# Square roots of the first three chunks by arithmetic on VectorE, with a new order of the operations

## The chip, the cores and the metric

The kernel runs on one core of a Trainium2 chip. The metric is the device time of one execution, in microseconds (us). The engines are called PE (TensorE; its weight loads are PEld), DVE (VectorE), ACT (ScalarE) and POOL (GpSimd); SP (SyncE) issues the DMAs. Each engine takes its own queue in program order and waits for others by semaphores.

## What is computed

A gated linear recurrence, followed by a gated convolution unit, over 4 sequences of 6336 tokens with 256 features:

```python
log_a = c * sig_r * np.log(np.clip(a_base, 1e-06, 1.0 - 1e-06))[None, None, :]
a_t = np.exp(log_a)
norm = np.sqrt(np.maximum(1.0 - a_t * a_t, 1e-06))
x_gated = norm * sig_i * x
for t in range(S):
    h = a_t[:, t] * h + x_gated[:, t]
    y[:, t] = h
# then, with x = y:
#   gate = sigmoid(causal convolution of x over 5 tokens, by feature)
#   out  = (gate * (x @ w_val)) @ w_out
```

`sig_r` and `sig_i` are the sigmoids of `r_gate` and `i_gate`. The change is about the square root in the third line.

## The kernel before

The 25,344 tokens are cut into 51 windows (`CHUNKS`, line 16): two of 256 tokens, then 48 of 512, and a last one of 256. Windows go in 28 chunks: chunks 0, 1 and 2 are the single windows 0, 1 and 2 (256, 256 and 512 tokens), and most of the others have two windows, so chunk 3 is windows 3 and 4.

Loads and stores are laid out with tokens on the partitions; the recurrence needs features on the partitions, in two halves of 128 (h = 0, 1). Each window or chunk goes through these steps; the two letters are their names in the order:

- `lr`, `li`, `lx` (L274): SP loads the r gate, the i gate and x of a window, 512 KB each for 512 tokens, into rings of four windows.
- `th` (L289): ACT takes tanh of both gates of a window at once, into `tring`, a ring of three windows. Of its three planes the i gate always lies in plane 1, and the r gate in plane 0 or 2 by turns.
- The i gate with x: POOL by `pp` (L297, adds 1) and `up` (L309, times x), or, for some windows, PE and DVE: `xp` (L314) brings x through PE into PSUM, and `uv` (L323) adds 1 and multiplies on DVE.
- `tr` (L334): PE transposes the r gate, one half of the features at a time; `ex` (L350): ACT takes exp with the feature's factor, which gives `a` in `aring`.
- The square of `a`, in `ering`: `sq` on POOL (L358) or `sa` on ACT (L366).
- `rt` (L377): ACT takes the root of a batch of chunks as Sqrt(0.25 - 0.25 * square), which is half of the norm, without the floor of 1e-6. tanh and exp lie in one table set and Sqrt in another, so ACT loads a table ahead of a batch of roots and another behind it (L509). `BATCHES` (line 19) says which chunks go together: 0, 1 and 2 each alone, then [3, 4], then three chunks at a time, and [26, 27].
- `nt` (L392): PE transposes the roots back; `xg` (L399): DVE multiplies them into the gated x; `xt` (L408): PE transposes the product; `sc` (L430): DVE runs the recurrence along the tokens, by chunk and half.
- Per window: `cv` (L442, the convolution as matmuls), `tg` (L449, tanh of it on ACT), `vl` (L457, x @ w_val), `gv` (L462, the gate on DVE), `ou` (L472, @ w_out), the copy out of PSUM by `cd` on DVE (L480) or `ca` on ACT (L482), and `st` (L493, the store).

The order of all this is the text `ORDER` (line 33), written out in advance: one word per step with the step's window or chunk, its half, and behind `@` the PSUM banks that it uses. A loop at the end (L504) emits the words one by one, so each engine's queue is the words of that engine in this order. Nothing is reordered later. The loop also puts in the table loads, wherever the next word of ACT needs the other set:

```python
table, have = {"th": EXP, "tg": EXP, "ex": EXP, "rt": SQRT}, EXP
if table.get(name, have) != have:
    have = table[name]
    nc.scalar.preload_act_table_set(have)
```

Of the kernel before, what the change touches and what calls it, by code (L numbers as in the profile page):

```python
# [38 lines left out]
s_wl.2 lr.8 li.10 lx.8 xt.2@2,3 xt.1@0,1 sc.1.1 li.9 lr.10 sq.3.0 rt.3 li.11 up.6 sc.1.0 lx.10 lr.11 sc.2.1 sc.2.0
up.5 th.8 lx.11 s_wcast th.10 lx.9 pp.10 up.10 lr.14 th.9 li.13 li.14 lr.13 xp.8@4,5 li.12 lr.12 uv.8 th.11 li.15  # L40
nt.3@0,1 xg.3 nt.4@6,7 pp.11 up.11 cv.1@2,3 tg.1 xg.4 xt.3@0,1 sc.3.1 vl.1@4,5 tr.5.0@6,7 ex.5.0 sq.5.0 tr.5.1@2,3
gv.1 ou.1.0@1 cd.1.0 st.1 lx.12 lr.15 ex.5.1 vl.0@4,5 xp.9@6,7 th.14 sq.5.1 cv.2@2,3 sc.3.0 th.13 uv.9 lx.13 xt.4@1,0
gv.0 ou.0.0@4 cd.0.0 st.0 sc.4.1 lx.15 cv.3@6,7 th.12 li.16 li.18 tr.7.1@4,5 tg.2 vl.2@2,3 gv.2 tg.3 ex.7.1 sq.6.1
sq.6.0 lx.14 pp.14 pp.12 up.12 tr.7.0@6,7 ex.7.0 sq.7.0 lx.16 cv.4@2,3 tg.4 th.15 ou.2.0@4,5 cd.2.0 sc.4.0 st.2 lr.18
lr.16 vl.3@6,7 xp.13@2,3 vl.4@4,5 gv.4 sq.7.1 rt.4 uv.13 th.16 sq.8.1 sq.8.0 pp.15 up.15 li.17 lr.17 up.14 ou.4.0@4,5
li.19 cv.5@0,1 lr.19 gv.3 cd.4.0 lx.17 tg.5 ou.3.0@6,7 lx.18 st.4 cd.3.0 st.3 nt.5@4,5 li.20 xg.5 pp.16 up.16 th.17
pp.17 lr.20 nt.7@6,7 xg.7 lx.19 li.21 nt.6@2,3 xg.6 th.18 pp.18 lr.21 xt.5@4,5 sc.5.1 up.17 vl.5@6,7 cv.6@0,1 tg.6
th.19 tr.9.1@2,3 ex.9.1 li.22 lr.22 up.18 sq.9.1 pp.19 gv.5 sc.5.0 tr.9.0@6,7 ex.9.0 lx.20 ou.5.0@0,1 cd.5.0 sq.10.1
xt.6@5,4 up.19 sc.6.1 cv.7@0,1 tg.7 cv.8@2,3 th.20 lr.24 tg.8 sc.6.0 vl.6@6,7 gv.6 xt.7@0,1 cv.9@4,5 ou.6.0@6,7 sc.7.0
th.21 tg.9 cd.6.0 vl.7@2,3 gv.7 vl.9@6,7 th.22 tr.11.0@0 sc.7.1 ou.7.0@2,3 vl.8@4,5 sq.9.0 tr.12.0@1 gv.9 ou.9.0@6,7  # L50
gv.8 ou.8.0@4,5 sq.10.0 st.5 cd.7.0 cd.9.0 lx.22 st.6 rt.5 lx.21 nt.8@6,7 lr.23 li.23 cd.8.0 nt.9@4,5 pp.22 pp.21
up.22 pp.20 up.20 up.21 xg.8 ex.12.0 xg.9 ex.11.0 li.24 st.7 st.9 li.25 lr.25 lx.23 lx.24 li.26 lr.26 th.23 xt.8@6,7
sc.8.0 sq.11.0 pp.23 sq.12.0 lr.27 li.27 cv.11@2,3 tg.11 cv.10@4,5 sc.8.1 cv.12@0,1 st.8 th.24 pp.24 tg.10 tg.12
vl.11@2,3 tr.11.1@6 ex.11.1 gv.11 vl.10@4,5 gv.10 th.25 xt.9@0,1 sc.9.0 tr.12.1@2 ex.12.1 ou.11.0@6,7 cd.11.0
ou.10.0@4,5 cd.10.0 cv.14@2,3 up.23 lx.25 lx.27 th.26 nt.10@6,7 sc.9.1 st.11 li.29 st.10 tg.14 tr.13.0@4,5 xg.10 up.24
sq.11.1 th.27 ex.13.0 tr.13.1@2,3 vl.12@0,1 gv.12 sq.12.1 li.30 lr.30 lx.26 pp.25 pp.27 sq.13.0 xt.10@6,7 sc.10.1
ex.13.1 sq.13.1 up.27 sq.14.0 pp.26 up.25 lr.28 cv.13@4,5 tg.13 vl.13@0,1 gv.13 li.28 vl.14@2,3 gv.14 ou.12.0@4,5
cd.12.0 ou.13.0@0,1 cd.13.0 ou.14.0@2,3 cv.15@4,5 lr.29 st.13 lx.28 lr.31 sc.10.0 cv.16@0,1 cd.14.0 rt.6 nt.11@6,7
tg.15 tg.16 xg.11 vl.15@2,3 gv.15 th.28 st.12 li.31 lx.29 sq.14.1 up.26 nt.13@4,5 xg.13 pp.28 up.28 nt.12@0,1 xg.12
li.32 vl.16@2,3 gv.16 lx.31 lr.32 lx.30 xt.11@4,5 sc.11.1 sc.11.0 ou.15.0@6,7 th.30 pp.30 th.29 pp.29 cv.18@0,1  # L60
ca.15.0 lr.34 li.34 up.29 cv.17@2,3 tg.18 xt.12@6,7 tg.17 vl.17@0,1 gv.17 tr.15.1@2,3 tr.15.0@4,5 th.31 sc.12.0
ou.17.0@0,1 cd.17.0 sc.12.1 ex.15.1 ex.15.0 cv.20@2,3 tg.20 li.33 lr.33 ou.16.0@0,1 cd.16.0 th.32 vl.18@4,5 gv.18
pp.31 up.31 th.34 xt.13@2,3 sc.13.1 vl.19@6,7 cv.19@0,1 tg.19 gv.19 st.17 st.14 st.16 st.15 up.30 th.33 sq.16.1 lx.32
sc.13.0 li.35 lr.35 lx.33 ou.18.0@4,5 cd.18.0 lx.34 li.36 sq.15.0 lr.38 cv.21@0,1 sq.15.1 vl.21@6,7 st.18 lx.35 lr.36
tg.21 gv.21 vl.20@0,1 sq.16.0 cv.22@2,3 gv.20 li.38 lr.37 li.37 pp.34 ou.19.0@4,5 cd.19.0 pp.33 pp.32 up.32
ou.21.0@6,7 ou.20.0@0,1 rt.7 cd.21.0 st.21 tg.22 cd.20.0 nt.14@4,5 xg.14 st.19 nt.16@6,7 xg.16 vl.22@0,1 gv.22 th.35
up.33 up.34 pp.35 tr.17.1@2,3 ex.17.1 xt.14@4,5 sc.14.0 sc.14.1 tr.17.0@6,7 ex.17.0 cv.23@0,1 cv.24@2,3 tg.23 tg.24
ou.22.0@6,7 cd.22.0 nt.15@0,1 xg.15 vl.24@2,3 vl.23@4,5 gv.23 st.20 st.22 lx.36 gv.24 up.35 cv.26@6,7 sq.17.1 th.36
pp.36 sq.18.0 th.38 xt.15@0,1 sc.15.0 sc.15.1 th.37 pp.37 sq.18.1 sq.17.0 ou.23.0@4,5 tg.26 ca.23.0 cv.25@2,3 tg.25
tr.19.0@6,7 ex.19.0 sq.19.0 xt.16@4,5 sc.16.0 tr.19.1@2,3 ex.19.1 sc.16.1 cv.27@0,1 ou.24.0@6,7 cd.24.0 tg.27  # L70
vl.25@2,3 vl.26@0,1 sq.19.1 rt.8 cv.28@4,5 gv.26 up.36 sq.20.1 li.39 st.23 lx.38 lr.40 pp.38 gv.25 lx.37 vl.27@6,7
gv.27 ou.26.0@0,1 cd.26.0 ou.25.0@2,3 lr.41 lr.39 tg.28 th.39 st.24 cd.25.0 ou.27.0@6,7 cd.27.0 nt.19@0,1 nt.17@2,3
xg.17 xg.19 cv.29@6,7 tg.29 sq.20.0 up.37 up.38 nt.18@4,5 xg.18 vl.28@2,3 gv.28 vl.29@6,7 gv.29 xt.17@0,1 sc.17.1
li.40 th.40 tr.21.1@4 li.41 th.41 pp.40 pp.39 st.26 st.25 tr.21.0@5 ex.21.1 ex.21.0 lx.39 li.42 ou.29.0@6,7 ca.29.0
lr.42 sc.17.0 st.27 lx.40 xt.18@2,3 up.39 th.42 ou.28.0@4,5 cv.30@6,7 cd.28.0 tg.30 tr.22.1@0 ex.22.1 tr.22.0@1
sq.21.0 sq.21.1 up.40 cv.32@6,7 ex.22.0 sq.22.1 tg.32 sc.18.1 cv.31@4,5 tg.31 lr.43 st.29 sc.18.0 li.43 th.43
vl.30@0,1 vl.31@6,7 gv.30 vl.32@4,5 gv.32 gv.31 ou.30.0@0,1 cd.30.0 xt.19@3,2 sc.19.0 ou.31.0@6,7 sq.22.0 rt.9
ou.32.0@4,5 st.28 cd.32.0 cd.31.0 lr.44 sc.19.1 lx.41 lx.43 lr.45 pp.42 pp.43 pp.41 up.41 li.44 up.43 lr.46 li.46
lx.42 up.42 st.30 cv.33@0,1 li.45 vl.33@4,5 tg.33 st.32 gv.33 nt.21@6,7 th.44 nt.20@0,1 xg.20 lx.45 lr.47 li.48 lr.48
th.46 pp.44 xg.21 nt.22@2,3 xg.22 lx.44 cv.35@4,5 th.45 pp.45 pp.46 up.45 st.31 li.47 ou.33.0@0,1 ca.33.0 tg.35  # L80
xt.20@6,7 sc.20.0 tr.23.1@2,3 ex.23.1 sc.20.1 cv.34@0,1 tg.34 cv.36@4,5 sq.24.1 tg.36 vl.35@2,3 gv.35 vl.36@0,1 gv.36
tr.23.0@6,7 vl.34@2,3 gv.34 ou.35.0@4,5 cd.35.0 lx.46 st.33 up.44 xt.21@0,1 sq.23.1 th.48 pp.48 ex.23.0 sq.24.0
sc.21.0 sc.21.1 th.47 cv.38@2,3 tg.38 ou.36.0@4,5 ou.34.0@6,7 ca.36.0 sq.23.0 ca.34.0 xt.22@2,3 tr.25.0@0 ex.25.0
sc.22.1 sq.25.0 tr.25.1@4 ex.25.1 sc.22.0 cv.37@6,7 tg.37 cv.39@0,1 tg.39 vl.40@4,5 vl.38@6,7 gv.38 sq.25.1 rt.10
st.35 li.49 st.36 vl.37@0,1 st.34 vl.39@2,3 lx.49 lr.49 lr.50 lx.48 gv.37 ou.38.0@6,7 cd.38.0 st.38 gv.39 cv.40@0,1
ou.37.0@6,7 cd.37.0 st.37 lx.47 nt.23@2,3 nt.24@6,7 tg.40 up.46 th.49 ou.39.0@0,1 ca.39.0 xg.23 xt.23@2,3 xg.24
cv.41@6,7 gv.40 ou.40.0@0,1 tg.41 ca.40.0 pp.49 pp.47 sc.23.1 cv.42@4,5 vl.41@0,1 sc.23.0 tg.42 gv.41 tr.26.0@3 li.50
ex.26.0 vl.42@6,7 st.39 up.47 th.50 xt.24@4,5 nt.25@2,3 gv.42 up.48 xg.25 st.40 ou.41.0@0,1 ca.41.0 st.41 cv.43@6,7
# [452 lines left out]
```

## Time and profile before

| | |
|---|---|
| median of 3 runs | 300.46 us (300.38 to 301.98) |
| the profiled execution | 300.32 us |
| its span in the trace | 298.5 us |
| ACT busy | 278.8 us, 93% of the span |
| DVE busy | 247.6 us, 83% |
| PE busy | 246.4 us, 83% |
| POOL busy | 232.8 us, 78% |
| DMA | 104.75 MB, mean 351 GB/s |

The span is the time from the first to the last instruction in the trace; 1.82 us of the execution lie around it. An engine's busy time is the time in which it had an instruction under way. In the profile's second part the span is cut into 40 equal slices, one digit each: the busy share of an engine in tenths. A row of a group gives line, engine, operation, what is written and read with its shape, the count, then busy us and the mean ns of one, then the idle time just before and what ended it. In a timeline, the first number is the start in us and the second the length.

### The profile page before, as it was taken

The page shows a single profiled execution, that of the slowest core. Times are in us where ns is not written, and L with a number is a line of the kernel's source. Part 1 is how long each engine was busy: PE and PEld are TensorE (multiplying, and loading weights), DVE is VectorE, ACT ScalarE, POOL GpSimd, SP SyncE. Part 2 cuts the span into 40 slices and gives each one's busy share as a digit, 9 for nine tenths or more (in the row PEclk, how much of TensorE's full clock was granted, in tenths as well). Part 3 has the DMA queues.
Part 4 walks back from the last instruction along what each step waited for, and adds up shares of the span by engine and source line. Part 5 has one row for each costly group of instructions (what it writes and reads, how often), then busy time and mean ns, then how long its engine had stood idle before and what let it go on. Part 6 is the DMA issues. An engine that isn't in the chain of part 4 may idle for free.

```text
span 298.5 us, 6286 instructions
## 1 busy us (share of the span) xinstructions
PE 246.4 (83%) x2509; PEld 167.8 (56%) x2509; DVE 247.6 (83%) x206; ACT 278.8 (93%) x197; POOL 232.8 (78%) x155
## 2 busy tenths in 40 slices
...
DVE  2030288849999889999999999999999899899993
ACT  6799999999999999999999999999999999969863
...
GB/s 252 408 408 385 379 411 407 406 414 406 337 379 370 419 416 415 411 406 321 417 411 375 388 417 335 396 353 361 349 409 419 408 278 270 273 116 248 29 186 246
DMA packets 29995, 104.75 MB, mean 351 GB/s; under 512 B 3335, under 2 KB 3854, under 8 KB 29966
## 3 DMA queue, kind: packets, MB, share of 16 engines
...
HBM read 78.39 MB, written 25.95 MB: 350 GB/s over the span
## 4 chain that ended last, share of the span: by engine, by line
ACT 31%; PE 23%; DVE 13%; issue 13%; DMA 12%; POOL 5%; SPq 1%; ACTq 0%; DVEq 0%; POOLq 0%
ACT tring L289 10%; ACT aring L350 8%; DMA riring<-in_r_gate_dram 7%; DVE yring L430 7%; PE banks L442 5%; ACT tgring L449 5%; PE banks L457 5%; ACT ering L377 4%; PE banks L472 4%; PE banks L392 3%; DMA riring<-in_i_gate_dram 3%; DVE tgring L462 3%; DVE oring L480 2%; DMA xring<-in_x_dram 2%; ACT L509 2%
## 5 line engine op out<-in xcount | busy, mean ns | idle before, releaser
L430 DVE TENSOR_TENSOR_SCAN yring<-aring,yring,banks 128x1024 bf16<-128x1024 f32 (+5 forms) x54 | 106.2, 1988 | 0.9 <-PE banks L408 0.6
L358 POOL TENSOR_TENSOR ering<-aring 128x1024 f32<-128x1024 f32 (+2 forms) x54 | 91.5, 1713 | 9.7 <-ACT aring L350 9.7
L309 POOL TENSOR_TENSOR uring<-tring,xring 128x1024 bf16<-128x1024 bf16 (+1 forms) x45 | 94.6, 2113 | 4.9 <-DMA xring<-in_x_dram 3.5
L289 ACT ACTIVATE tring<-riring 128x2048 bf16<-128x2048 f32 (+1 forms) x51 | 93.8, 1867 | 4.1 <-DMA riring<-in_i_gate_dram 1.9
L297 POOL TENSOR_SCALAR tring<-tring 128x1024 bf16<-128x1024 bf16 (+1 forms) x45 | 45.8, 1026 | 30.5 <-ACT tring L289 30.4
L442 PE MATMUL banks<-yring,diag 64*64 64x512 bf16 (+7 forms) x1080 | 61.9, 361 | 4.6 <-ACT aring L350 1.6
L462 DVE SCALAR_TENSOR_TENSOR tgring<-tgring,banks 128x1024 bf16<-128x1024 bf16 (+1 forms) x51 | 58.9, 1178 | 5.5 <-PE banks L457 4.4
L472 PE MATMUL banks<-wo,tgring 128*128 128x256 bf16 x396 | 51.4, 274 | 4.7 <-DVE tgring L462 3.5
L350 ACT ACTIVATE aring<-banks,khf 128x2048 f32<-128x2048 bf16 (+3 forms) x38 | 54.1, 1474 | 0.5 <-PE banks L334 0.4
L449 ACT ACTIVATE tgring<-banks 128x1024 bf16<-128x1024 f32 (+1 forms) x51 | 50.4, 1009 | 3.4 <-PE banks L442 3.3
L457 PE MATMUL banks<-yring,wv 128*128 128x512 bf16 (+4 forms) x216 | 49.4, 361 | 5.0 <-DVE oring L480 2.2
L472 PEld LDWEIGHTS <-tgring 128*128 128x128 bf16 x396 | 41.0, 114 | 15.7 <-DVE tgring L462 9.6
L442 PEld LDWEIGHTS <-diag 64*64 64x64 bf16 x1080 | 30.3, 106 | 28.8 <-issue 13.6
L377 ACT ACTIVATE ering<-ering 128x4096 bf16<-128x4096 f32 (+5 forms) x15 | 44.9, 3019 | 0.1
L399 DVE TENSOR_TENSOR uring<-banks,uring 128x2048 bf16<-128x2048 bf16 (+2 forms) x28 | 29.8, 1095 | 18.2 <-PE banks L392 17.9
L480 DVE COPY oring<-banks 128x1024 f32<-128x1024 f32 (+1 forms) x35 | 40.6, 1181 | 4.8 <-ACT aring L350 2.4
L334 PE MATMUL banks<-ident_b,tring 128*128 128x128 bf16 x396 | 29.0, 227 | 12.2 <-ACT tring L289 10.4
L334 PEld LDWEIGHTS <-tring 128*128 128x128 bf16 x396 | 25.1, 101 | 17.7 <-ACT tring L289 11.7
L457 PEld LDWEIGHTS <-wv 128*128 128x128 bf16 x216 | 19.7, 97 | 26.3 <-issue 12.4
L392 PE MATMUL banks<-ident,ering 128*128 128x128 f32 x198 | 28.8, 296 | 6.8 <-DVE oring L480 2.6
L392 PEld LDWEIGHTS banks<-ident,ering 128*128 128x128 f32 x198 | 25.9, 208 | 13.5 <-ACT ering L377 7.7
L408 PE MATMUL banks<-ident,uring 128*128 128x128 f32 x198 | 27.5, 282 | 2.6 <-DVE uring L399 2.5
...
## 6 DMA issues: line engine op xcount, KB each, us to landing
...
```

The source lines that it names most:

```text
L289: nc.scalar.activation(out=tring[:, w % NTRI, a:a + 2, 0:J, :], in_=riring[:, w % NRI, :, 0:J, :], func=ACT.Tanh, scale=0.5)
L309: nc.gpsimd.tensor_tensor(out=u, in0=t1, in1=xt, op=ALU.mult)
L350: nc.scalar.activation(out=dst, in_=src, func=ACT.Exp, scale=khf[:, h:h + 1], bias=khf[:, h:h + 1])
L358: nc.gpsimd.tensor_tensor(out=e, in0=a, in1=a, op=ALU.mult)
L377: nc.scalar.activation(out=ering[:].bitcast(BF16)[:, 4 * o:4 * o + 2 * n], in_=ering[:, 2 * o:2 * o + 2 * n], func=ACT.Sqrt, scale=-0.25, ...
L392: nc.tensor.transpose(out=bank[:, k:k + P], in_=ering[:, e + q:e + wins[w] // 2:nq], identity=ident[:])
L430: nc.vector.tensor_tensor_scan(out=yring[:, h, col:col + o1 - o0], data0=aring[:, h, a_at[c] + o0:a_at[c] + o1], data1=xT[:, o0:o1], initi ...
L442: nc.tensor.matmul(out=gp[oh * 64:oh * 64 + 64, h, a:b], lhsT=diag[half * 64:half * 64 + 64, h, k, :], rhs=yring[half * 64:half * 64 + 64, ...
L449: nc.scalar.activation(out=tgring[:, w % NTG, :, 0:wins[w]], in_=live.pop(("gp", w))[:, :, 0:wins[w]], func=ACT.Tanh, scale=0.5)
L457: nc.tensor.matmul(out=val[:, m, a:b], lhsT=wv[:, hk, m * P:(m + 1) * P], rhs=yring[:, hk, col:col + b - a], start=(hk == 0), stop=(hk == ...
L462: nc.vector.scalar_tensor_tensor(out=tgring[:, w % NTG, :, 0:wins[w]], in0=tgring[:, w % NTG, :, 0:wins[w]], scalar=1.0, in1=live.pop(("va ...
L472: nc.tensor.matmul(out=ops[:, j * D:(j + 1) * D], lhsT=gv[:, hk, j:wins[w]:J], rhs=wo[:, hk, :], start=(hk == 0), stop=(hk == H - 1))
```

## The change

The roots of chunks 0, 1 and 2 leave ACT. Two new steps do them. `nx` on POOL takes the square, in place, to min(square - 1, -1e-6): the negative of the number under the root, with the reference's floor. `nr` on DVE takes the root of a piece of 512 columns in seven operations: the first reads the number's bits as an integer and makes a first guess of the reciprocal root out of them, and six `scalar_tensor_tensor` operations refine it and multiply it out, with results by turns in PSUM banks and in two slots of `oring` that no store uses yet. Chunks 0 and 1 need one `nr` each, chunk 2 needs two. The words `rt.0`, `rt.1` and `rt.2` are gone; `rt.3` to `rt.11` remain, computed as before.

The order is new as a whole, from its first words to its last. In it, two more squares are on ACT (`sa.0.0` and `sa.2.0`; `sa.3.0` stands where `sa.4.0` was), windows 4, 7, 9, 11 and 13 go by `xp` and `uv` instead of 3, 1, 7, 8, 9 and 13, and so POOL has 46 `pp` and `up` instead of 45. The numbers of `th`, `ex`, `tg`, `ca`, `sc`, `gv` and `cd` are the same.

```diff
+INT32 = mybir.dt.int32
...
+ROOT_SEED = float(0x5F1FFFF9 - (1 << 30))
+ROOT_A = 0.703952253
+ROOT_B = 2.38924456
...
 ORDER = """
-s_ident s_small s_kt s_diag li.2 lr.2 th.2 lr.3 lr.0 li.0 th.0 pp.0 tr.2.0@0 li.1 lr.1 tr.0.0@1 ex.2.0 th.1 lx.0 lx.2
-li.3 up.0 tr.2.1@2 ex.2.1 tr.0.1@0 ex.0.0 tr.1.1@3 ex.1.1 tr.1.0@4 sq.1.1 ex.0.1 sq.0.1 lx.3 xp.3@0,1 lx.1 lr.6 th.3
-sq.0.0 rt.0 lr.5 sq.2.0 pp.2 up.2 nt.0@5 xg.0 xt.0@2,3 li.5 th.5 sq.2.1 li.6 lr.4 uv.3 th.6 pp.6 pp.5 xp.1@5 sc.0.0
-sc.0.1 cv.0@2,3 uv.1 li.4 th.4 tg.0 s_wl.1 ex.1.0 lx.4 li.7 tr.3.1@0,1 s_wl.0 lr.7 ex.3.1 lx.5 tr.3.0@2,3 ex.3.0
...
+s_ident s_small s_kt s_diag lx.3 li.0 lr.0 th.0 li.2 lr.2 tr.0.0@0 ex.0.0 lx.2 lx.0 lr.1 tr.0.1@1 lx.1 ex.0.1 sa.0.0
+li.1 th.2 sq.0.1 nx.0 nr.0.0@0,1 tr.2.1@2 pp.0 pp.2 up.0 li.3 th.1 pp.1 lr.3 lr.4 li.4 tr.1.1@3 nt.0@0 tr.2.0@1 ex.1.1
+up.2 sq.1.1 xg.0 tr.1.0@3 lx.4 ex.1.0 sq.1.0 up.1 nx.1 ex.2.1 th.3 xt.0@4,5 ex.2.0 sa.2.0 th.4 pp.3 up.3 nr.1.0@0,1
+sc.0.1 lr.6 li.6 th.6 lr.5 li.5 th.5 li.7 lr.7 xp.4@2,3 tr.3.1@0,1 uv.4 tr.3.0@2,3 th.7 nt.1@5 ex.3.1 ex.3.0 lx.5 li.8
+lr.8 lx.8 lx.7 xp.7@2,3 sq.2.1 nx.2 nr.2.0@6,7 xg.1 xt.1@0,1 sc.0.0 nr.2.1@6,7 uv.7 nt.2@6 sc.1.0 pp.5 up.5 th.8
+sq.3.1 sq.4.1 sq.4.0 cv.0@4,5 xg.2 xt.2@2,3 lr.9 lr.10 s_wl.3 li.9 li.11 sa.3.0 pp.8 rt.3 lx.6 li.10 th.10 pp.6 up.8
+up.6 th.9 sc.1.1 cv.1@0,1 nt.3@6,7 tg.0 tg.1 s_wl.0 lr.12 s_wl.2 s_wl.1 lx.9 sc.2.1 sc.2.0 cv.2@2,3 lx.11 xg.3
...
+        def op_nx(b):
+            c, = BATCHES[b]
+            e = ering[:, H * e_at[c]:H * (e_at[c] + clen[c])]
+            nc.gpsimd.tensor_scalar(out=e, in0=e, scalar1=1.0, scalar2=-1e-6, op0=ALU.subtract, op1=ALU.min)
+            live["n", c] = H * e_at[c]
+
+        def op_nr(b, k, *at):
+            c, = BATCHES[b]
+            o, n = H * e_at[c] + 512 * k, 512
+            minus = ering[:, o:o + n]
+            y, t = banks[:, at[0]], banks[:, at[1]]
+            g = oring[:, 1].rearrange("p j d -> p (j d)")[:, k * n:(k + 1) * n]
+            u = oring[:, 2].rearrange("p j d -> p (j d)")[:, k * n:(k + 1) * n]
+            half = ering[:].bitcast(BF16)[:, 4 * e_at[c] + k * n:4 * e_at[c] + (k + 1) * n]
+            nc.vector.tensor_scalar(out=y.bitcast(INT32), in0=minus.bitcast(INT32), scalar1=-0.5, scalar2=ROOT_SEED,
+                                    op0=ALU.mult, op1=ALU.add)
+            stt = nc.vector.scalar_tensor_tensor
+            stt(out=g, in0=minus, scalar=-0.5, in1=y, op0=ALU.mult, op1=ALU.mult)
+            stt(out=t, in0=g, scalar=-2.0 * ROOT_A, in1=y, op0=ALU.mult, op1=ALU.mult)
+            stt(out=g, in0=t, scalar=ROOT_A * ROOT_B, in1=g, op0=ALU.add, op1=ALU.mult)
+            stt(out=u, in0=g, scalar=-1.0, in1=y, op0=ALU.mult, op1=ALU.mult)
+            stt(out=t, in0=t, scalar=ROOT_A * ROOT_B, in1=u, op0=ALU.add, op1=ALU.mult)
+            stt(out=half, in0=t, scalar=1.5, in1=g, op0=ALU.add, op1=ALU.mult)
```

More of the change, by code (lines that the diff above doesn't have):

```diff
@@ L39 @@
[L39 to L88, printed above, removed]
@@ new lines @@
+lr.8 lx.8 lx.7 xp.7@2,3 sq.2.1 nx.2 nr.2.0@6,7 xg.1 xt.1@0,1 sc.0.0 nr.2.1@6,7 uv.7 nt.2@6 sc.1.0 pp.5 up.5 th.8
+sq.3.1 sq.4.1 sq.4.0 cv.0@4,5 xg.2 xt.2@2,3 lr.9 lr.10 s_wl.3 li.9 li.11 sa.3.0 pp.8 rt.3 lx.6 li.10 th.10 pp.6 up.8
+up.6 th.9 sc.1.1 cv.1@0,1 nt.3@6,7 tg.0 tg.1 s_wl.0 lr.12 s_wl.2 s_wl.1 lx.9 sc.2.1 sc.2.0 cv.2@2,3 lx.11 xg.3
+xt.3@6,7 sc.3.1 sc.3.0 tg.2 tr.5.1@4,5 ex.5.1 tr.5.0@0,1 lr.11 xp.9@2,3 pp.10 lx.10 li.12 lr.13 li.13 lr.14 xp.11@4,5
+li.14 lx.12 uv.9 lx.13 th.11 ex.5.0 uv.11 th.12 li.15 s_wcast vl.1@6,7 gv.1 sq.6.1 nt.4@2,3 vl.0@0,1 vl.2@4,5 gv.0
@@ new lines @@
+ou.1.0@6 gv.2 up.10 th.13 ou.0.0@7 lx.14 cd.0.0 cd.1.0 st.0 lr.15 st.1 th.14 cv.4@0,1 cv.3@4,5 tg.3 lx.15 li.18 tg.4
+xg.4 lr.16 sq.5.0 sq.6.0 vl.3@6,7 tr.7.0@2,3 gv.3 ex.7.0 xt.4@4,5 lr.17 pp.12 sq.5.1 sc.4.0 tr.7.1@0,1 ex.7.1 up.12
+ou.2.0@6,7 cd.2.0 st.2 li.16 th.15 sq.7.0 lr.18 li.17 ou.3.0@2,3 xp.13@6,7 vl.4@0,1 sc.4.1 cd.3.0 li.19 pp.14 sq.7.1
+lx.16 gv.4 ou.4.0@0,1 cd.4.0 pp.15 up.14 sq.8.1 uv.13 vl.5@2,3 st.3 lr.19 cv.5@4,5 lx.17 rt.4 nt.5@6,7 xg.5 tg.5
+nt.6@0,1 gv.5 th.16 cv.6@4,5 st.4 sq.8.0 lx.18 xg.6 ou.5.0@2,3 cd.5.0 up.15 xt.5@6,7 sc.5.0 pp.16 up.16 th.17 th.18
@@ new lines @@
+lr.21 st.5 li.21 sc.5.1 vl.6@0,1 li.20 tg.6 gv.6 lr.20 th.19 li.23 lr.22 lx.20 lx.19 tr.9.1@2,3 tr.9.0@4,5 xt.6@6,7
+sc.6.1 sc.6.0 ex.9.0 ex.9.1 pp.17 pp.18 cv.7@0,1 tg.7 cv.8@4,5 vl.7@2,3 gv.7 up.17 tg.8 up.18 th.21 ou.6.0@0,1 cd.6.0
+st.6 nt.7@4,5 vl.8@6,7 xg.7 cv.9@2,3 xt.7@4,5 gv.8 lr.23 ou.7.0@0,1 li.22 sq.10.0 vl.9@6,7 sq.10.1 sq.9.0 sq.9.1 lx.21
+sc.7.0 cd.7.0 th.20 tr.11.0@4 lr.24 cv.10@0,1 tg.9 gv.9 st.7 lx.22 li.24 vl.10@6,7 pp.19 pp.21 up.19 lx.23 pp.20
+sc.7.1 up.20 ou.9.0@2,3 cd.9.0 st.9 rt.5 nt.8@2,3 tg.10 gv.10 lr.25 up.21 th.22 pp.22 xg.8 ou.8.0@0,1 li.26 li.25
@@ new lines @@
+cd.8.0 lr.26 ou.10.0@6,7 cd.10.0 ex.11.0 nt.9@2,3 xg.9 lx.24 tr.12.0@4 sq.11.0 th.23 lx.25 st.8 xt.8@0,1 sc.8.0 sc.8.1
+ex.12.0 th.24 lr.28 pp.23 up.22 up.23 li.27 lr.27 pp.24 tr.12.1@5 ex.12.1 xt.9@2,3 tr.11.1@4 ex.11.1 cv.11@6,7 tg.11
+li.28 sq.12.1 th.25 pp.25 up.24 vl.11@4,5 gv.11 sc.9.1 cv.13@6,7 th.26 cv.12@0,1 tg.12 tr.13.1@4,5 tg.13 vl.12@0,1
+ex.13.1 tr.13.0@6,7 sc.9.0 ex.13.0 gv.12 st.10 lx.27 ou.11.0@2,3 cd.11.0 nt.10@0,1 xg.10 ou.12.0@4,5 vl.14@2,3 cd.12.0
+xt.10@0,1 sc.10.1 st.11 lx.26 st.12 lr.29 up.25 sq.11.1 sq.13.1 sq.13.0 sq.12.0 lx.28 li.30 li.29 th.27 pp.26 sq.14.0
@@ new lines @@
+pp.27 th.28 cv.15@6,7 tg.15 up.26 cv.14@4,5 tg.14 vl.15@6,7 vl.13@4,5 sc.10.0 cv.18@0,1 lr.30 gv.15 ou.15.0@6,7 rt.6
+gv.14 ou.14.0@2,3 gv.13 cd.15.0 li.31 ou.13.0@4,5 cd.13.0 st.15 st.13 lx.30 cv.16@6,7 tg.16 cd.14.0 nt.11@4,5 xg.11
+nt.12@2,3 xg.12 nt.13@6,7 xg.13 pp.28 up.27 lr.31 xt.11@4,5 sc.11.0 th.29 up.28 sq.14.1 th.30 cv.17@2,3 tg.17 lx.29
+pp.30 pp.29 lr.33 li.33 tg.18 tr.15.0@6,7 up.30 lr.32 li.32 up.29 sc.11.1 ex.15.0 sq.15.0 vl.18@2,3 th.31 vl.16@0,1
+gv.16 tr.15.1@4,5 ex.15.1 sq.16.1 sq.15.1 sq.16.0 st.14 gv.18 lr.34 lx.31 lx.33 th.33 pp.33 vl.17@6,7 gv.17 xt.12@0,1
```

43 lines of the change are left out of this document (34 added, 9 removed).

## The prediction

> **What bounds the kernel now.** I read the page's first two parts, then the ACT groups with shapes kept apart, then the timelines of ACT and DVE up to 75 us, then the table of 10 us stretches.
>
> From the page:
>
> ```profile
> PE 246.4 (83%) x2509; PEld 167.8 (56%) x2509; DVE 247.6 (83%) x206; ACT 278.8 (93%) x197; POOL 232.8 (78%) x155
> ...
> DVE  2030288849999889999999999999999899899993
> ACT  6799999999999999999999999999999999969863
> ```
>
> ACT is full from the second slice to about 258 us; PE and DVE fill the tail. DVE has holes only in its first five slices. From the 10 us stretches, two of the later ones (behind the length of the stretch, busy us of PE, PEld, DVE, ACT, POOL, each with its count):
>
> ```profile
> 150.00:160.00 10.00, 9.25 (x91) 5.35 (x84) 10.00 (x7) 9.98 (x8) 10.00 (x6) 1.00 1.02 390
> 220.00:230.00 10.00, 7.88 (x80) 5.70 (x69) 10.00 (x10) 9.97 (x7) 6.73 (x4) 1.00 1.03 412
> ```
>
> So after the start DVE is as full as ACT: from 80 to 250 us ACT is idle 0.9 us in all by these rows, DVE 5.5 us. Time saved on ACT alone is worth little there, and time saved at the start counts only if it is still there when this full stretch begins. I take the table load before `rt.4` (67.53 us) as that point.
>
> The ACT timeline of the start (start, length, and in brackets the wait before):
>
> ```profile
> 5.58 1.91 ACT L289 ACTIVATE tring<-riring 128x2048 bf16<-128x2048 f32 x1 [0.83 <-DMA riring<-in_r_gate_dram]
> 9.22 1.06 ACT L289 ACTIVATE tring<-riring 128x1024 bf16<-128x1024 f32 x1 [1.73 <-DMA riring<-in_i_gate_dram]
> ...
> 15.80 1.28 ACT L509 ACT_TABLE_LOAD   x1
> 17.10 0.63 ACT L377 ACTIVATE ering<-ering 128x512 bf16<-128x512 f32 x1
> 17.75 1.28 ACT L509 ACT_TABLE_LOAD   x1
> 19.57 3.71 ACT L289 ACTIVATE tring<-riring 128x2048 bf16<-128x2048 f32 x2 [0.54 <-POOL uring L309]
> 23.46 1.91 ACT L289 ACTIVATE tring<-riring 128x2048 bf16<-128x2048 f32 x1 [0.18 <-DMA riring<-in_i_gate_dram]
> ...
> 67.53 1.28 ACT L509 ACT_TABLE_LOAD   x1
> ```
>
> The reader is to see the pair of loads around a root of 0.63 us, and that ACT, from 5.58 to 67.53, waits only some 3 us.
>
> **What leaves ACT.** The built queue of the changed kernel has 18 loads at the root switches, not 20, so the change does on ACT what it says. From the groups by shape:
>
> ```profile
> L509 ACT ACT_TABLE_LOAD x20 | 25.7, 1283 | 0.4
> L377 ACT ACTIVATE ering<-ering 128x512 bf16<-128x512 f32 x2 | 1.2, 622 | 0.0
> L377 ACT ACTIVATE ering<-ering 128x1024 bf16<-128x1024 f32 x1 | 1.1, 1057 | 0.0
> L366 ACT ACTIVATE ering<-aring 128x1024 f32<-128x1024 f32 x1 | 1.0, 1040 | 0.0
> L366 ACT ACTIVATE ering<-aring 128x256 f32<-128x256 f32 x1 | 0.4, 419 | 0.0
> ```
>
> Gone: `rt.0`, `rt.1` (2 x 0.62), `rt.2` (1.06), two loads (2 x 1.28): 4.87 us. New: two squares, `sa.0.0` with 256 columns (0.42) and `sa.2.0` with 512, between 0.42 and 1.04; on the line through both rows 0.63. (`sa.3.0` takes the place of `sa.4.0`.) Net: 3.8 us less on ACT. The root of chunks 3 and 4 keeps its pair.
>
> The Trainium skill, "ScalarE: Activation LUTs", section "What ACT_TABLE_LOAD costs", puts a drain of 1.38 us behind each load of 1.28, so two loads would be worth 5.3 us. In this trace the root starts at 17.10, 0.02 us after its load ends (15.80 + 1.28): no such drain is seen. By the rule the net would be 6.6 us; I keep the row.
>
> **What DVE gets.** Four chains `nr` (chunk 0, chunk 1, two halves of chunk 2), seven operations of 512 fp32 columns each, 28 in all, one input or the output in PSUM. No row has this form; the nearest are
>
> ```profile
> L323 DVE SCALAR_TENSOR_TENSOR uring<-tring,banks 128x512 bf16<-128x512 bf16 x11 | 7.6, 732 | 13.1 <-PE banks L314 12.8 <-ACT tring L289 0.3
> L480 DVE COPY oring<-banks 128x512 f32<-128x512 f32 x2 | 1.4, 692 | 1.6 <-PE banks L472 1.6
> ```
>
> Below, a short operation without dependence starts before the one ahead has ended (pairs of L323 take 1.35, so 0.63 apart); above, 0.73 plus 0.03 between dependent ones (L225 to L226: 2.64 + 0.17 to 2.84), or 0.76. Farther out lies the scan of 512 columns at 1.257, another kind of work. I take 0.70, nearest to the fp32 copy: 4.9 us a chain, 19.6 in all, 17.6 to 21.3 by the bounds. One `uv` call less takes 0.7 off.
>
> The Trainium skill, "VectorE: DVE Perf Modes", section on the TRN2 errata, gives 120 cycles plus one per column at 0.96 GHz from PSUM, an estimate of 0.66 us here, below the rows of 0.68 to 0.73; by it the chains would take 18.4 us.
>
> In the before, DVE waited 13.6 us ahead of 19.45 and 12.0 ahead of 34.95, so the room is there, though not where it is needed.
>
> **What POOL gets.** One `pp` and one `up` (1.05 + 2.16), three `nx` of 512, 512 and 1024 fp32 columns, against the squares that moved to ACT (0.61 + 1.04). An `nx` of 512 lies between `pp` of 512 (0.62) and the weight scaling at L260 (1.49); I take the fp32 square's 1.04, and 1.90 for 1024. Net +5.5 us. POOL had waited 8.7 us at the start, but `up` and `nx` now release others.
>
> **The start, worked out.** Arrivals: two transfers of 512 KB (1.0 MB) are there at 5.58, 2.0 MB at 9.22, 4.25 MB at 15.1 (first L314), 7.5 MB at 23.46 (`li.4`): 3.6 us for the second MB, then 2.6 each. The new queue on SP is lx.3 li.0 lr.0 li.2 lr.2 lx.2 lx.0 lr.1 lx.1 li.1 ...: `th.0` has its 1.0 MB at 5.6, `th.2` its 2.0 at 9.2, `th.1` its 3.5 at 13.1. (Before, `th.1` needed 2.5 MB.) Then, with ex 0.56, 0.77 or 2.0, th 1.05 or 1.85 apart:
>
> - ACT: th.0 5.6 to 6.65; transposes; ex.0.0, ex.0.1, sa.0.0 7.05 to 8.5; **wait to 9.2**; th.2 to 11.1; **wait to 13.1**; th.1 to 14.15; ex.1.1 14.5 to 15.05.
> - POOL squares the other half of chunk 0 and does nx.0 by 9.9. DVE: nr.0.0 9.9 to 14.8. PE's queue holds nt.0 behind it, and behind that tr.2.0 and tr.1.0 (15.8). So ACT **waits to 15.9** for ex.1.0; ex.2.1, th.3, ex.2.0, sa.2.0, th.4 to 22.1.
> - POOL: up.2 must have th.2's gate and comes after pp.1 (14.75), so up.2 ends at 16.9, squares and up.1 at 19.25, nx.1 20.3, pp.3 and up.3 23.5. th.6 overwrites the plane up.3 reads: ACT **waits to 23.5**. Then th.6, th.5, th.7 (uv.4 is done at 27.2, just in time), ex.3.1, ex.3.0, th.8, sa.3.0 to 35.9, load, rt.3, load: back in the exp set at 42.1.
>
> Before, the same point is 40.87 plus `th.8` (1.85) less `tg.0` (0.5): 42.2. The waits are 0.4 + 0.7 + 2.0 + 0.4 + 0.85 + 1.4 = 5.8 us against 2.5 in the before: they eat 3.3 of the 3.8 saved (the rest is rounding of overlaps).
>
> - DVE runs nr.1.0 20.3 to 25.2, nr.2.0 27.2 to 32.1, nr.2.1 33.2 to 38.1, then with no pause the scans of chunks 0 to 2 to 43.8 and xg.3 to 45.0 (before: xg.3 at 44.07). PE: tr.5 by 48, two xp of 2 us each, vl.1 at 52 (before 46.3), cv.3 just before 60. ACT reaches tg.3 at 59.5: no wait, or a short one.
>
> So the load before `rt.4` comes at 67.3 against 67.53. Up to there both orders have given ACT the same 16 th, 12 ex and 5 tg and DVE the same 10 scans; from xg.5 on DVE's work is the same list of kinds in another order. 300.32 (the profiled execution: span 298.5 plus 1.82 around it; the median of the runs is 300.46) less 0.2 is **300.1 us**.
>
> **Rivals.**
> - *Faster, 0.28.* My waits are too long: transfers of the small chunks land earlier, or nx costs 0.62 and up.3 frees th.6 sooner. At best all 3.8 us stay: 296.5. Half of them, 298.2, is likelier. For it: POOL and the loads stand one or two windows further at `rt.4` in the new order. Against it: DVE has 5.5 us idle in 170, so it can't follow much. The drain of the ScalarE page would add 2.8 to this; its chance is 0.02, within the 0.28.
> - *Slower, 0.30: DVE becomes the bound between 20 and 60 us.* At 0.85 a step instead of 0.70 the chains take 28 x 0.15 = 4.2 us more; DVE has no gap from 20 to 54 us, PE takes xt.3, tr.5 and vl.1 in order behind it, and tg.3 waits for cv.3. It decides from about 0.72 a step, where cv.3 ends after th.14. The time is then 300.1 + 28 x 0.13 = 303.7. For it: the full rows of DVE later, which give nothing back. Against: no 512-column row but the scan is over 0.73.
> - *No change, 0.42*, the forecast: saved work turned into waits, within 0.5% (1.5 us, about what a measurement of this kernel can tell from no change).
>
> The range takes half of the best gain and a bit more at the low end (297.0) and the slow rival at the high end (304.0). A step as dear as the scan's 1.257 (28 x 0.55 = 15 us more) is left outside.
>
> **What would show it.** In the trace after: ACT waits of about 2 us ahead of the second 1024-column tanh (DMA) and 1.4 us ahead of a tanh (POOL uring); 18 loads; 28 DVE operations of 0.65 to 0.76; the load before `rt.4` within 1 us of 67.3. Wrong would be: ACT dense from 6 us on (faster), DVE operations over 0.8 or ACT waiting for PE at L449's counterpart near 60 us (slower), or a changed sum of ACT or DVE idle time after 75 us, which comes of the new order and which I put at nothing.

## The result, and the profile after

The changed kernel takes 302.81 us (median of 22 runs), the kernel before in the same sessions 301.57 us (22 runs). The ratio of the times is 1.0049, with a 95% interval of 1.0028 to 1.0071: slower by about 1.5 us. (Over 22 runs the kernel before comes out 1.1 us above the three runs of the table further up; a run of either kernel varies by about 1 us, so only the ratio is used from here on.) The profiled execution took 303.62 us with a span of 301.8, so the two traces lie 3.3 us apart, more than the ratio says: one is a little above its median, the other below. Of the old order with nx on POOL, the last run below, four of twelve executions, the traced one among them, fell into a slower state and are left out.

The page of the changed kernel, engines and slices:

```profile
PE 247.0 (82%) x2482; PEld 168.5 (56%) x2507; DVE 265.4 (88%) x233; ACT 274.7 (91%) x194; POOL 240.1 (80%) x158
...
DVE  2247897988799989999999999999999899999993
ACT  3647998999999999999999999999998999989643
```

ACT lost 4.1 us of work and is nevertheless emptier at the start: its first four slices were 6, 7, 9, 9 and are now 3, 6, 4, 7. DVE, which began with 2, 0, 3, 0, 2, now begins with 2, 2, 4, 7, 8. Two later stretches (length, then busy us of PE, PEld, DVE, ACT, POOL):

```profile
150.00:160.00 10.00, 9.10 (x93) 5.98 (x92) 10.00 (x8) 9.98 (x8) 10.00 (x6) 1.00 1.01 389
220.00:230.00 10.00, 8.16 (x82) 5.42 (x82) 10.00 (x8) 9.96 (x7) 7.63 (x5) 1.00 1.02 381
```

They are as full as before. ACT's start (start, length, in brackets the wait before):

```profile
7.53 1.06 ACT L294 ACTIVATE tring<-riring 128x1024 bf16<-128x1024 f32 x1 [2.79 <-DMA riring<-in_r_gate_dram]
...
14.05 1.06 ACT L294 ACTIVATE tring<-riring 128x1024 bf16<-128x1024 f32 x1 [1.85 <-DMA riring<-in_i_gate_dram]
...
19.45 1.23 ACT L355 ACTIVATE aring<-banks,khf 128x256 f32<-128x256 bf16 x2 [3.28 <-PE banks L339]
...
27.21 5.62 ACT L294 ACTIVATE tring<-riring 128x2048 bf16<-128x2048 f32 x3 [1.60 <-POOL uring L314]
...
71.52 1.28 ACT L538 ACT_TABLE_LOAD   x1
```

The rows are th.0, th.1, ex.1.0 with the exp after it, th.6 with the two after it, and the load ahead of rt.4. That load stood at 67.53 and stands at 71.52: the whole loss of the trace is there by then, 4.0 us, which is more than the 1.5 us of the ratio. From it to the end of the span there are 230.3 us, against 231.0 before.

POOL in the same time:

```profile
10.88 1.93 POOL L391 TENSOR_SCALAR ering<-ering 128x512 f32<-128x512 f32 x1
...
21.91 1.92 POOL L391 TENSOR_SCALAR ering<-ering 128x512 f32<-128x512 f32 x1
23.91 1.04 POOL L302 TENSOR_SCALAR tring<-tring 128x1024 bf16<-128x1024 bf16 x1
25.03 2.14 POOL L314 TENSOR_TENSOR uring<-tring,xring 128x1024 bf16<-128x1024 bf16 x1
...
28.25 3.63 POOL L391 TENSOR_SCALAR ering<-ering 128x1024 f32<-128x1024 f32 x1
```

Here are the three nx (L391) of 1.93, 1.92 and 3.63 us, and behind the second pp.3 and up.3, which ends at 27.17. ACT's th.6 starts at 27.21. On DVE the steps of nr are short; two of the seven lines by shape:

```profile
L402 DVE TENSOR_SCALAR banks<-ering 128x512 int32<-128x512 int32 x4 | 2.8, 688 | 13.2 <-POOL ering L391 13.2
L405 DVE SCALAR_TENSOR_TENSOR oring<-ering,banks 128x512 f32<-128x512 f32 x4 | 2.7, 687 | 0.1
```

The other five take 687 to 699 ns; a chain starts a step every 0.73 us. DVE waits 13.2 us, all for nx.

### The profile page after: what moved, and what is told of

It is laid out like the page before. It is cut to its first block, busy times and chain, and to the rows that moved or that the text cites. A ratio compares the mean times of both kernels' runs of the same rounds, so it can differ in the third digit from the quotient of the medians.

```text
span 301.8 us, 6296 instructions
## 1 busy us (share of the span) xinstructions
PE 247.0 (82%) x2482; PEld 168.5 (56%) x2507; DVE 265.4 (88%) x233; ACT 274.7 (91%) x194; POOL 240.1 (80%) x158
## 4 chain that ended last, share of the span: by engine, by line
PE 26%; POOL 21%; DVE 18%; ACT 13%; issue 12%; DMA 8%; SPq 0%; DVEq 0%; ACTq 0%; POOLq 0%
POOL uring L314 8%; POOL ering L363 6%; PE banks L471 6%; PE banks L501 5%; DVE yring L459 5%; PE banks L486 5%; DMA riring<-in_r_gate_dram 5%; POOL tring L302 4%; ACT tgring L478 4%; PE banks L421 3%; DMA out_dram<-oring 3%; DVE tgring L491 3%; DVE oring L509 3%; PE banks L437 3%; ACT ering L382 3%
## 5 line engine op out<-in xcount | busy, mean ns | idle before, releaser
L363 POOL TENSOR_TENSOR ering<-aring 128x1024 f32<-128x1024 f32 (+2 forms) x52 | 89.8, 1745 | 18.9 <-ACT aring L355 18.7
L314 POOL TENSOR_TENSOR uring<-tring,xring 128x1024 bf16<-128x1024 bf16 (+1 forms) x46 | 95.6, 2091 | 5.2 <-DMA xring<-in_x_dram 3.3
L471 PE MATMUL banks<-yring,diag 64*64 64x512 bf16 (+7 forms) x1080 | 63.1, 367 | 4.8 <-DVE oring L509 1.6
L486 PE MATMUL banks<-yring,wv 128*128 128x512 bf16 (+7 forms) x191 | 48.0, 358 | 5.8 <-ACT tgring L478 2.5
L501 PEld LDWEIGHTS <-tgring 128*128 128x128 bf16 x396 | 41.7, 114 | 12.8 <-DVE tgring L491 7.1
L339 PE MATMUL banks<-ident_b,tring 128*128 128x128 bf16 x396 | 30.8, 230 | 19.5 <-ACT tring L294 12.0
L382 ACT ACTIVATE ering<-ering 128x4096 bf16<-128x4096 f32 (+3 forms) x12 | 42.7, 3581 | 0.1
L339 PEld LDWEIGHTS <-tring 128*128 128x128 bf16 x396 | 26.2, 103 | 26.6 <-ACT tring L294 13.2
L421 PE MATMUL banks<-ident,ering 128*128 128x128 f32 x198 | 31.0, 301 | 8.3 <-DVE ering L410 3.4
L421 PEld LDWEIGHTS banks<-ident,ering 128*128 128x128 f32 x198 | 26.6, 208 | 15.0 <-issue 8.2
L486 PEld LDWEIGHTS <-wv 128*128 128x128 bf16 x216 | 19.9, 97 | 25.1 <-issue 11.3
```

The source lines that it names most:

```text
L314: nc.gpsimd.tensor_tensor(out=u, in0=t1, in1=xt, op=ALU.mult)
L339: nc.tensor.transpose(out=bank[:, o:o + P], in_=tring[:, w % NTRI, 2 * swapped(w), j, h * P:(h + 1) * P], identity=ident_b[:])
L363: nc.gpsimd.tensor_tensor(out=e, in0=a, in1=a, op=ALU.mult)
L421: nc.tensor.transpose(out=bank[:, k:k + P], in_=ering[:, e + q:e + wins[w] // 2:nq], identity=ident[:])
L471: nc.tensor.matmul(out=gp[oh * 64:oh * 64 + 64, h, a:b], lhsT=diag[half * 64:half * 64 + 64, h, k, :], rhs=yring[half * 64:half * 64 + 64, ...
L486: nc.tensor.matmul(out=val[:, m, a:b], lhsT=wv[:, hk, m * P:(m + 1) * P], rhs=yring[:, hk, col:col + b - a], start=(hk == 0), stop=(hk == ...
```

## The experiments

Theory A, after the traces: all the loss is made in the first 28 us. It runs through the arrival of the first gates, nx.0, the first nr chain and the transposes behind it, and above all through POOL: nx.1, pp.3, up.3, th.6. Rival C: DVE, with 18 us more work, fills the full stretch from 80 us on, and would take back whatever the start gives.

Read from the traces, in us; "rest" is the span less the load ahead of rt.4; the ratio is to the kernel before, from 4 to 12 runs of each experiment and 21 to 31 of the kernel before in the same sessions:

| run | th.0 | first nr | th.6 | load ahead of rt.4 | rest | ratio (95%) |
|---|---|---|---|---|---|---|
| before | | | 21.4 | 67.5 | 231.0 | 1 |
| changed | 7.5 | 12.8 | 27.2 | 71.5 | 230.3 | 1.0049 (1.0028 to 1.0071) |
| x load later | 5.5 | 10.8 | 25.1 | 70.3 | 229.4 | 0.999 (0.996 to 1.002) |
| nx on DVE | 6.4 | 10.7 | 23.7 | 66.6 | 229.7 | 0.9927 (0.9898 to 0.9956) |
| tr.1.0 first | 7.1 | 12.4 | 25.6 | 70.0 | 229.3 | 1.0003 (0.9976 to 1.003) |
| these three | 4.8 | 9.0 | 23.0 | 67.2 | 230.1 | 0.9931 (0.9899 to 0.9964) |
| no floor | 7.0 | 11.0 | 24.0 | 67.1 | 229.8 | 0.9899 (0.9855 to 0.9943) |
| nx on DVE, tr.1.0 first | 6.0 | 10.2 | 22.7 | 66.7 | 230.5 | 0.9881 (0.9845 to 0.9917) |
| plus, min | 7.9 | | 27.6 | 71.4 | 229.3 | 1.0045 (1.002 to 1.007) |
| minus, plus 0 | 7.3 | | 26.8 | 72.0 | 229.3 | 1.0051 (1.0012 to 1.0091) |
| nx.2 on DVE | 6.2 | 11.5 | 25.9 | 69.7 | 229.3 | 1.0005 (0.9978 to 1.0032) |
| nx.0, nx.1 on DVE | 7.7 | 11.9 | 24.9 | 70.0 | 229.7 | 0.9948 (0.9919 to 0.9977) |
| old order, nx.0 on DVE | | 16.2 | 23.9 | 69.8 | 232.6 | 1.0071 (1.0033 to 1.0109) |
| old order, nx.0 on POOL | | | | | | 1.0056 (1.0022 to 1.0091) |

th.0 scatters: with lx.3, li.0 and lr.0 first in the queue it starts anywhere from 6.0 to 7.9 (the rows of the new order but the two with the x load later). So times are compared by the ratios, and the traces for what waits on what.

**The x load of window 3 later.**

```diff
-s_diag lx.3 li.0 lr.0 ... pp.1 lr.3 lr.4 li.4
+s_diag li.0 lr.0 ... pp.1 lr.3 lx.3 lr.4 li.4
```

> The changed kernel with one load moved: x of window 3 no longer leads SP's queue but stands behind the r gate of window 3. Theory A (the start decides: the wait of 2.8 us for the first gates and the POOL chain behind it push all that follows): the first tanh of 1024 columns starts at 5.5 instead of 7.5 us, the first nr operation at 11 instead of 12.8, the table load before rt.4 at 69.6 instead of 71.5, and the time falls by about 2 us, to within 0.2% of the kernel before. Rival B (small transfers of 256 KB are slow to land wherever they stand): the first tanh stays at or above 7 us and the time stays. Rival C (DVE, with 18 us more work, fills the rest and takes back what the start gives): the first tanh is earlier, the load before rt.4 too, and the time stays within 0.5 us of the changed kernel.

th.0 starts at 5.45, now right behind its table load, and the first nr at 10.77. The load ahead of rt.4 moves by 1.3 us and not 1.9: near 50 us tg.2 now waits 1.25 for PE, where it waited 0.27. The ratio moves to 0.999, 0.6% less than the changed kernel's. Theory A fits; small transfers are not slow in themselves, and C gives nothing back.

**nx on DVE.**

```diff
-            nc.gpsimd.tensor_scalar(out=e, in0=e, scalar1=1.0, scalar2=-1e-6, op0=ALU.subtract, op1=ALU.min)
+            nc.vector.tensor_scalar(out=e, in0=e, scalar1=1.0, scalar2=-1e-6, op0=ALU.subtract, op1=ALU.min)
```

> The changed kernel with the three nx operations on DVE instead of POOL, nothing else. Theory A (nx took 1.92, 1.92 and 3.63 us on POOL, twice the estimate, and up.3 behind it lets th.6 start only at 27.2): POOL loses 7.5 us, DVE gains three operations of 0.4 to 0.7 us each for 512 columns; the first nr operation starts near 11.3, th.6 near 24, the load before rt.4 near 68.5, and the time falls by 3 us, about 0.5% below the kernel before. Rival C (DVE fills the rest): th.6 is earlier, yet the time stays within 0.5 us of the changed kernel or rises, since DVE has 1.6 us more.

```profile
23.65 5.51 ACT L294 ACTIVATE tring<-riring 128x2048 bf16<-128x2048 f32 x3 [0.27 <-POOL uring L314]
...
66.59 1.28 ACT L538 ACT_TABLE_LOAD   x1
```

th.6 comes at 23.65 and its wait for up.3 is 0.27 us, and the load ahead of rt.4 at 66.59, earlier than the 68.5 of the expectation. The time is 1.2% under the changed kernel and 0.7% under the kernel before: more than twice the loss goes when this one step changes its engine. DVE has the 18 us of the change and nx on top (268.1 us busy), and still the rest is 229.7 us: rival C falls.

**tr.1.0 ahead of nt.0.**

```diff
-tr.1.1@3 nt.0@0 tr.2.0@1 ex.1.1 up.2 sq.1.1 xg.0 tr.1.0@3
+tr.1.1@3 ex.1.1 tr.1.0@3 nt.0@0 tr.2.0@1 up.2 sq.1.1 xg.0
```

> The changed kernel with the transposes tr.1.0 ahead of nt.0 and tr.2.0 in PE's queue, so that they don't stand behind the wait for the first nr chain. Theory A: ex.1.0 starts at 16.2 instead of 19.5 (ACT's wait of 3.3 us goes), but th.6 is set by POOL's chain of nx.1, pp.3 and up.3, which gains only the 1.2 us that POOL waited for ex.1.0: th.6 at 26.0, the load before rt.4 at 70.3, time 1.2 us less. Rival D (the wait for PE is what costs, so all of its 3.3 us come back): load before rt.4 at 68.3, time 3 us less. Rival C: no change of the time.

ex.1.0 starts at 16.23 and its wait falls from 3.28 to 0.46; but now ACT waits 3.17 ahead of th.6 for up.3, where it had waited 1.60. The gain is 0.46%, 1.4 us, near the 1.2 that POOL had waited and less than half of the 3 us of rival D. So the longest wait in ACT's timeline was not the one that counted: what came behind it was held by POOL.

**The three together.**

> All three edits: the load of x of window 3 later, nx on DVE, tr.1.0 ahead of nt.0. Theory A: the gains of the start add up as far as the loads allow: th.6 near 22.5, the load before rt.4 near 66.5, 5 us earlier than in the changed kernel, the time near 0.988 of the kernel before. Rival C (DVE's full stretch from 80 us on takes it back): the load before rt.4 as early, but the time not under 0.997 of the kernel before.

A miss for the sum: 0.9931, no better than nx on DVE alone. The three tanh th.6, th.5 and th.7 show where it went:

```profile
22.97 1.91 ACT L294 ACTIVATE tring<-riring 128x2048 bf16<-128x2048 f32 x1 [1.53 <-DMA riring<-in_i_gate_dram]
25.51 1.91 ACT L294 ACTIVATE tring<-riring 128x2048 bf16<-128x2048 f32 x1 [0.63 <-DMA riring<-in_i_gate_dram]
28.09 1.91 ACT L294 ACTIVATE tring<-riring 128x2048 bf16<-128x2048 f32 x1 [0.67 <-DMA riring<-in_r_gate_dram]
```

Each waits for gates that haven't landed: with POOL out of the way the loads are next. It is not C either: the load ahead of rt.4 is itself only at 67.15.

**nx on DVE and tr.1.0 first, the x load where the change has it.**

> The changed kernel with nx on DVE and tr.1.0 ahead of nt.0, and the load of x of window 3 left where the change put it. In the run with all three edits ACT waited 2.8 us in all for gate loads of windows 6, 5 and 7, which the run with nx on DVE alone did not. If the moved load did that, this run has no such waits over 0.5 us, ex.1.0 starts 2 us earlier than with nx on DVE alone, th.6 starts at 23.2 to 23.6 and the load before rt.4 at 66.0 to 66.6: time equal to nx on DVE alone within 0.5 us. If the loads as a whole are the bound there, the waits for them appear here too, and the time is the same again.

Of the three waits for gates one is left (th.7, 0.67), so most of the 2.8 came of moving the x load. th.6 is at 22.72, the load ahead of rt.4 at 66.68. The ratio is 0.9881 (0.9845 to 0.9917): with the floor kept, 1.2% under the kernel before and clear of both kernels. Its interval overlaps that of nx on DVE alone, so whether tr.1.0 adds anything there is not shown; equal within 0.5 us was expected, and 1.4 us less was measured.

**nx with the operators of pp, without the floor.**

```diff
-scalar1=1.0, scalar2=-1e-6, op0=ALU.subtract, op1=ALU.min
+scalar1=1.0, scalar2=-1.0, op0=ALU.mult, op1=ALU.add
```

> The changed kernel with nx on POOL as before it, but as times 1.0 plus -1.0: the same subtraction written with the two operators of pp, and the floor left out. It asks why nx takes 1.92 us for 512 columns where the square takes 1.04 and pp, in bf16, 0.62. Theory E (the fp32 form of a POOL tensor_scalar is slow, whatever its operators): nx stays at 1.9 and 3.6 us and the time stays at 1.005 of the kernel before. Rival F (the operators of the floor are slow): nx falls to 1.0 us or less for 512 columns, and the time falls by 1 us or more.

Its three nx by shape:

```profile
L391 POOL TENSOR_SCALAR ering<-ering 128x512 f32<-128x512 f32 x2 | 1.2, 616 | 0.1
L391 POOL TENSOR_SCALAR ering<-ering 128x1024 f32<-128x1024 f32 x1 | 1.0, 1044 | 0.1
```

Rival F is right: same engine, same type, same columns, and 0.62 us instead of 1.92. The time is 0.9899 of the kernel before, 1.5% under the changed kernel: with the nx at this price, and on the same engine, the loss is gone.

**Which of the two operators.** First plus -1.0, then min with -1e-6; then minus 1.0, plus 0.0, without the floor.

> The changed kernel with nx on POOL written as plus -1.0, then min with -1e-6: the floor is kept and the subtraction becomes an addition. Without floor and subtraction nx took 0.62 us for 512 columns, with both 1.92. If the subtraction is the slow operator, nx is at 0.62 and 1.04 us here and the time is 0.99 of the kernel before; if the min is, nx stays at 1.9 and 3.6 us and the time near 1.005; if each costs its part, nx lies at about 1.2 us and the time near 0.997.

> The changed kernel with nx on POOL as minus 1.0 and then plus 0.0, the floor left out: the subtraction alone. The other half of the question: if the subtraction is slow, nx stays at 1.9 us for 512 columns; if the min is, it falls to 0.62.

The first of them:

```profile
L391 POOL TENSOR_SCALAR ering<-ering 128x512 f32<-128x512 f32 x2 | 3.9, 1927 | 0.2
```

The second gives 1928 ns. So it is not one operator that is slow: plus with min is slow, minus with plus is slow, only times with plus was fast. Whether minus and min are each slow, or only the pair of times and plus is fast, these runs do not separate; of the pairs tried, none with the floor was fast.

They also answer a rival that the traces suggest. Between 28 and 75 us the granted clock of PE was 0.91 before and 0.78 in the changed kernel. With plus and min it was 1.00, and still the load ahead of rt.4 comes 63.5 us after th.0. In the changed kernel these are 64.0 us, and only 60.2 with nx on DVE, where the clock was 0.84: the clock did not make the loss.

**Which of the three nx.** On DVE only nx.2, or only nx.0 and nx.1.

> The changed kernel with only nx.2 (1024 columns, 3.63 us on POOL) on DVE; nx.0 and nx.1 stay on POOL. If the cost runs through nx.0 and nx.1, up.3 and th.6, this changes little: th.6 stays near 27 us, the first operation of nr.2.0 comes at 31.5 instead of 31.9, the load before rt.4 stays at 71 to 71.5, ratio 1.002 to 1.005. If POOL's sum of work is what costs, half of it is taken away here, and the ratio falls to about 0.998.

> The changed kernel with nx.0 and nx.1 on DVE and nx.2 on POOL, where it takes 3.63 us. If the cost runs through nx.0 and nx.1, up.3 and th.6, nearly all comes back: th.6 near 23.7, the load before rt.4 near 66.6 to 67.5, ratio 0.992 to 0.995. If POOL's sum of work is what costs, about half comes back, ratio near 0.998.

nx.0 and nx.1 give back 1.0% of the time, nx.2 alone 0.44%: the first as expected by the chain through up.3, the second a little more than by that chain alone. But the load ahead of rt.4 comes at 70.0 with nx.0 and nx.1 moved, not at 66.6 to 67.5 as expected. The root rt.3 waits 0.18 there for a square of POOL behind nx.2, and the chain nr.2.0 waits 1.49 for nx.2; tg.2 and ex.5.1 then wait for PE:

```profile
49.39 1.02 ACT L479 ACTIVATE tgring<-banks 128x1024 bf16<-128x1024 f32 x1 [1.24 <-PE banks L472]
51.29 2.06 ACT L355 ACTIVATE aring<-banks,khf 128x2048 f32<-128x2048 bf16 x1 [0.87 <-PE banks L339]
```

In the changed kernel these two waits are 0.27 and 1.06, with all nx on DVE none and 0.20. Counted from th.0, the load comes after 64.0 us in the changed kernel, 62.3 with nx.0 and nx.1 moved, 63.5 with nx.2 moved and 60.2 with all three. So the largest nx was in part hidden behind the two small ones, and theory A is too narrow: a part of the loss is made by nx.2, behind the first 28 us.

**The old order, only chunk 0's root on DVE.** In the order of the kernel before, rt.0 is replaced by nx.0 and nr.0.0 in banks 6 and 7, with nx on DVE or on POOL:

```diff
-sq.0.0 rt.0 lr.5 sq.2.0 pp.2 up.2
+sq.0.0 nx.0 nr.0.0@6,7 lr.5 sq.2.0 pp.2 up.2
```

> The order of the kernel before, with one step changed: the root of chunk 0 alone is taken off ACT, by nx on DVE and one nr chain of 5.1 us on DVE in the same place of the order; rt.1 and rt.2 stay on ACT. ACT loses two table loads and a root, 3.2 us. Theory G (at this place ACT has nothing else to do: th.5 can't start before up.2 is done on POOL at 19.5): ACT waits from 15.8 to 19.5 instead, uv.3 comes behind the chain on DVE, about 1 us later than before, and with it th.6; time 0 to 1 us more than the kernel before. Rival H (a table load less is a load's time won): 3.2 us less, ratio 0.99.

> As the run with the old order and nx on DVE, but with nx on POOL, where it stands ahead of sq.2.0, pp.2 and up.2. By theory A a POOL step of 1.9 us in the way of up.2 moves th.5 and all behind it by 1.9 us: th.5 at 21.5 instead of 19.6, the load before rt.4 near 69.5, time 2 to 3 us more than the kernel before. If nx on POOL were harmless, the two runs with the old order would be equal.

With nx on DVE the ratio is 1.0071 (1.0033 to 1.0109), 2.1 us more where 0 to 1 was expected, and ACT's start, th.5 and then th.6 with the one after it:

```profile
19.37 1.91 ACT L294 ACTIVATE tring<-riring 128x2048 bf16<-128x2048 f32 x1 [3.95 <-POOL uring L314]
23.89 3.85 ACT L294 ACTIVATE tring<-riring 128x2048 bf16<-128x2048 f32 x2 [2.61 <-DVE yring L448]
```

The 3.2 us of ACT that the root and its loads took turn into a wait of 3.95 for up.2, as theory G has it; and th.6 comes 2.5 us later than before, behind uv.3 and the chain ahead of it on DVE, where 1 was expected. With nx on POOL the ratio is 1.0056 (1.0022 to 1.0091), 1.7 us more: not the further 1.9 us that I expected. The two runs with the old order are equal within their intervals, and by the expectation's own sign nx on POOL did no harm in this place. That speaks against theory A here; without a trace to go by, why is left open.

## Why the prediction was wrong

The forecast was no change, 300.1 us; measured is 0.49% more, a small but clear loss. That the time lies inside the range of 297.0 to 304.0 is luck: the upper end came from the rival with DVE as the bound, which is not what happened.

- *What leaves ACT*: right. 18 loads of 1283 ns, sa.2.0 at 0.63 as interpolated; busy time fell by 4.1 us for 3.8.
- *What DVE gets*: right. 0.69 us a step, 0.73 apart, for 0.70; a chain of 5.1 us for 4.9.
- *What POOL gets*: this step failed. "An nx of 512 lies between pp of 512 (0.62) and the weight scaling at L260 (1.49); I take the fp32 square's 1.04, and 1.90 for 1024." Measured are 1.92 and 3.63, outside the bound. POOL's busy time rose by 7.3 us for 5.5, and would have risen by more if the added pp and up were not those of window 1, with 512 columns and 1.8 us together, where 3.2 were put. pp looked like the same kind of operation and was the exception; L260, one operation per element and still 1.49, was the row to go by.
- *The start, worked out*: the chain was named rightly, with up.3 ahead of th.6, nt.0 ahead of tr.1.0 and the waits for gates, and the sizes were off. The waits named as signs came (1.85 for the loads, 1.60 for up.3), and so did 18 loads; the load within 1 us of 67.3 did not. th.0 came at 7.53 instead of 5.6 and th.6 at 27.21 instead of 23.5. From th.0 to the load ahead of rt.4 I had 61.7 us; it took 64.0, and with the fast nx 60.1. On the line between these two, the forecast's price of nx gives 61.4, an estimate near the 61.7. So of the 4.2 us between 67.3 and 71.52, about 2.3 are nx and 1.9 the late first gates. Where the queue leads with lx.3, th.0 started at 6.0 to 7.9 in nine traces, never at the 5.6 that I took over from two other transfers.
- *The rest identical*: not shown. It took 229.3 to 230.5 us in every trace of the new order, 231.0 before and 232.6 in the old order with nx on DVE, so there is no sign that DVE's added work cost anything there. But it came out 0.5 to 1.7 us shorter than in the one trace of the kernel before, and three runs of the new order (the x load later, tr.1.0 first, nx.2 on DVE) take the time of the kernel before although their load ahead of rt.4 comes 2 to 3 us later. In the new order two more ou and cd stand ahead of rt.4 (five each, not three), which the forecast's list of equal work left out; that they are the reason is not shown.
- *The sum*: on the line between 0.9899 with the fast nx and 1.0049, the forecast's price of nx would give about 0.995 of the time before, an estimate. So the price of nx turned a small gain into a small loss, and at the forecast's price no change would probably have missed the other way.
- *Rivals*: the faster one named nx at 0.62 as a condition; the run without the floor fulfils it, and its 0.99 is near the 298.2 us that this rival gave. In the changed kernel nx was dearer, not cheaper. The slower one, DVE as the bound from 0.72 a step, is not what happened: DVE started a step every 0.73 us, just beyond that limit, but it waited 13.2 us for POOL, and with nx on DVE the same 28 steps go with a gain.

The Trainium skill, "GPSIMD Engine Reference", section "Engine selection", has one-input work on GPSIMD at roughly line rate. pp (0.62 us for 512 columns, 1.04 for 1024, so about 0.8 ns for each further column) and nx as times and plus (the same) fit that; nx with its floor, at 1.92 and 3.63, so 3.3 ns for each further column, does not, and the measurement decides.
